# A linear-attention and mixture-of-experts kernel: reordered opening, two added products, loads spread over marks, masks earlier in the vector queue

## The chip, the cores and the metric

The kernel runs on one core of a Trainium2 chip. A core has a matrix engine (PE, with its weight loads shown as PEld), a vector engine (DVE), a scalar engine (ACT), a general engine (POOL) and a queue engine (SP) that issues most transfers. Each engine takes its instructions in the order of its own queue; semaphores order the engines among each other. The metric is device time in microseconds (us) of one execution, as a median over runs.

## The reference

Two blocks stand one after the other. The first is a delta-rule attention over 4 batches x 8 heads (32 states), 768 positions, head size 48; its output is laid out as 3072 tokens of 384 numbers. The second is a mixture of 16 experts, of which each token takes one.

```python
k_n = k / (norm(k) + 1e-06)
for t in range(768):                       # each of the 32 heads has a 48 x 48 state
    y[t]  = q[t] @ state
    v_old = state^T k_n[t]
    state = state + beta[t] * outer(k_n[t], v[t] - v_old)
x = y as (3072, 384)
g = argmax(x @ w_group); e = argmax(x @ w_expert[g])          # 4 groups of 4 experts
out[token] = softmax weight of g * softmax weight of e * (relu(x @ w1[g, e]) @ w2[g, e])
```

Everything is computed in fp32.

## The kernel before, in words

The attention goes by chunks of 32 positions: 24 chunks (`NCH`), each for all 32 heads at once (4 batches x 32 positions = 128 partitions, 8 heads along the free side). Inside a chunk the recurrence is turned into a triangular solve: the matrix of products of a chunk's keys is inverted once, and then the chunk is a few matrix products with the running state `s_bd`.

For a chunk `u` the work is:

- `gram(u)` (line 234): 32 small PE products of keys with keys and queries (line 251), copied out by ACT into `gts` (line 256, input of the inverse) and `raws` (line 262, input of the mask). In the steady loop it runs ten chunks ahead (`LEAD`).
- `inverse(g)` (line 273): one inverse for a group of four chunks (`RG`), six groups in all, almost all of it on DVE. It begins with a transpose into `m` (L279) and the start of the roots (L287, for groups after the first). The norms' roots are 14 small POOL operations (L290 to L295) for the groups 1 to 5, and DVE operations for group 0. Then come the factor (L320 to L328), a product of 1024 columns (L330), the elimination in about ninety small steps (L338 to L366), two products of 1024 columns (L369, L372), the diagonal (L374), a transpose into `mt` (L377), and eight "spreads" of `mt` into `mtb` (lines 385 to 388; all on ACT except the first one of group 0, which is DVE's, L386). `inverse` is a generator; its `yield`s say what it stands at: `ROOTS` after the POOL operations are issued, `FACTOR` after the factor, `TURN` until the group before has been transposed.
- `scale(u)` (L403, DVE): the values times the norms, into `vh` (two buffers). It needs the norms of the chunk's group and the chunk's `kv` load.
- `mask(u)` (L268, DVE): the query products times a triangle, into `gqm` (three buffers).
- `advance(u)` (line 410), four steps: `a_ps` (PE, L416 from `vh` and L422 from the state, then ACT L426 to `f`) and the first part of `o_ps` (L431); `w_ps` (L439, from `f` and `mtb`; ACT L442); the new state (`s_ps` L449, copied to `s_bd` by ACT L455); the rest of `o_ps` (L463 or L468, from `gqm`), copied to `x` by ACT L472.
- `logits(u)` and `route(r)`: the router of the chunk's 128 tokens, a sorting of tokens by expert.

The order on every engine is written out by hand: within the `manual_schedule` block the instructions stand in each engine's queue in the order in which the Python code issues them. `work(n)` (line 663) issues DVE steps of the running inverses and routes for a budget that grows with `n` and with the task's share; `allow(what)` (line 676) pushes the tasks that stand at `what`.

The opening, before the loop over the chunks (lines 689 to 723): loads of the first keys; the gram products of chunks 0 to 7; `inverse(0)` by `work` calls; `scale(0)`; three small POOL operations (`acc`, `what`, `sel`); the first step of `advance(0)` (one product, L416); the gram products of chunks 8 and 9; then `inverse(1)` is started while the end of `inverse(0)` is still being issued, and `mask(0)` and `scale(1)` are issued when `mt` of group 0 has been issued.

The loads of the opening stand in `bursts` (line 221): after the i-th gram an ACT operation writes one element of the target (a "mark", L696), and the loads issued by SP wait for the mark, since they overwrite it. The last entry, after gram 10, marks and issues the loads of keys 8 and 9, `kv` 2, the router's weights `wr`, and keys 10 and 11.

At the end of a loop period `u` (lines 829 to 836): `mask(u + 1)`, `scale(u + 2)`, the loads of keys `u + 12` and `kv` `u + 3`, then the store of `x` of chunk `u`.

After the last chunk the experts' stage goes through the 16 experts in order of their token counts (L964 first layer, L983 second layer, weights loaded ahead, tokens gathered and results scattered by POOL's indirect transfers). The change touches none of it.

## Time and profile before

| what | value |
| --- | --- |
| median of 5 runs | 518.11 us (513.5 to 520.34) |
| the profiled execution, whole | 517.32 us |
| its span, first to last instruction | 515.1 us |
| PE busy over the span | 474.1 us (92%) |
| DVE busy over the span | 250.0 us (49%) |
| first `w_ps` of chunk 0 (L439) | starts at 42.95 us |
| last `w_ps`, chunk 23 | starts at 226.54 us |
| experts' stage, first L964 in the chain | from 243.08 us |

Times inside the profile are counted from the span's start. The page cuts the span into 40 slices of 12.9 us, so that a digit string shows where an engine is busy: the opening is the first three slices and a bit, the chunks reach to about the eighteenth, and the rest is the experts' stage. A wait is given as the engine and line that waited, what it waited for, the total, how often, and the longest. "issue" stands for idle time in which the engine waited for nothing that the profile shows. Rows of the timeline give start, duration, engine, line, operation, output and inputs, and in square brackets the idle time before.

### The profile page before, as it was taken

How to read it: one execution, taken by the hardware profiler on the slowest of the kernel's cores; microseconds unless marked ns; L12 is line 12 of the kernel's file. 1: busy time of each engine (PE TensorE's matmuls, PEld its weight loads, DVE VectorE, ACT ScalarE, POOL GpSimd, SP SyncE). 2: the span in 40 equal slices, each digit the busy share in tenths (PEclk: the TensorE clock that was granted, in tenths of full speed). 3: DMA queues.
4: the chain of work that ended last, by engine and by line, in shares of the span. 5: the costliest groups of instructions: out<-in, count | busy, mean ns of one | idle time of the engine just before them, and what ended most of it. 6: DMA issues, size and time to landing. Idle time of an engine off the chain costs nothing.

```text
span 515.1 us, 18246 instructions
## 1 busy us (share of the span) xinstructions
PE 474.1 (92%) x7844; PEld 439.1 (85%) x7844; DVE 250.0 (49%) x829; ACT 188.6 (37%) x397; POOL 194.4 (38%) x288
## 2 busy tenths in 40 slices
PE   4346999999999999999999999999999999999993
PEld 3235878878888788879999999999999999999992
DVE  3999999999999994426411022012201111011110
ACT  3224767677676776742111111111111121111110
POOL 0040200623717334010345554466435644454313
PEclk9999999999999999999999999999999999999998
DMA  5781444444324545210698877779768977879641
GB/s 176 251 296 44 153 145 140 166 147 156 132 70 131 158 142 184 71 45 17 160 363 255 264 260 255 224 229 315 251 193 280 334 244 243 262 272 307 216 166 46
DMA packets 57333, 99.94 MB, mean 194 GB/s; under 512 B 18974, under 2 KB 41433, under 8 KB 57251
## 3 DMA queue, kind: packets, MB, share of 16 engines
q1 hardware_dynamic: 51331, 88.76, 52.2%
q0 software_dynamic: 5920, 10.00, 6.2%
q8 instruction: 63, 1.03, 0.8%
q14 instruction: 19, 0.16, 0.1%
HBM read 84.61 MB, written 14.27 MB: 192 GB/s over the span
## 4 chain that ended last, share of the span: by engine, by line
PE 56%; issue 12%; DMA 10%; POOL 9%; DVE 5%; ACT 5%; SPq 1%; POOLq 0%; ACTq 0%; DVEq 0%
PE y_ps L983 12%; PE h_ps L964 12%; DMA out_dram<-yo,to_i 6%; POOL xq L936 6%; PE w_ps L439 5%; PE s_ps L449 5%; ACT s_bd L455 3%; PE a_ps L422 3%; PE l_ps L500 3%; PE o_ps L431 3%; PE o_ps L463 3%; PE g_ps L251 2%; PE t_ps L490 2%; PE a_ps L416 2%; POOL out_dram L995 2%
## 5 line engine op out<-in xcount | busy, mean ns | idle before, releaser
L983 PE MATMUL y_ps<-hid,w 128*128 128x224 f32 (+15 forms) x768 | 133.3, 332 | 0.7 <-issue 0.7
L983 PEld LDWEIGHTS y_ps<-hid,w 128*128 128x128 f32 x768 | 128.9, 190 | 2.2 <-issue 1.6
L964 PE MATMUL h_ps<-xt,w 128*128 128x232 f32 (+14 forms) x720 | 122.8, 330 | 0.0
L964 PEld LDWEIGHTS h_ps<-xt,w 128*128 128x128 f32 x720 | 120.0, 190 | 0.6 <-DVE xt L930 0.4
L936 POOL DMA_INDIRECT xq<-x_dram,from_q x92 | 87.8, 955 | 34.9 <-issue 24.8
L986 DVE COPY yt<-y_ps 128x232 f32<-128x232 f32 (+13 forms) x14 | 5.1, 366 | 135.9 <-PE y_ps L983 129.5
L995 POOL DMA_INDIRECT out_dram<-yo,to_i x32 | 34.2, 1067 | 94.2 <-DVE yo L1033 85.2
L967 ACT ACTIVATE hid<-h_ps 128x448 f32<-128x448 f32 (+15 forms) x64 | 32.1, 502 | 99.9 <-PE h_ps L964 80.6
L988 ACT ACTIVATE yt<-y_ps 128x224 f32<-128x224 f32 (+15 forms) x34 | 11.5, 337 | 119.1 <-PE y_ps L983 70.5
L366 DVE TENSOR_TENSOR m<-m,t 128x81 f32<-128x81 f32 (+13 forms) x156 | 52.1, 334 | 0.0
L360 DVE TENSOR_TENSOR t<-m 128x81 f32<-128x81 f32 (+13 forms) x156 | 51.8, 332 | 0.2
L455 ACT ACTIVATE s_bd<-s_ps 48x768 f32<-48x768 f32 x46 | 37.0, 804 | 14.0 <-PE s_ps L449 13.4
L343 DVE SCALAR_TENSOR_TENSOR m<-m 128x29 f32<-128x29 f32 (+27 forms) x174 | 40.4, 235 | 0.4
L1033 DVE TENSOR_SCALAR yo<-yr,gate 128x384 f32<-128x384 f32 (+14 forms) x28 | 11.1, 417 | 52.4 <-DMA yr<-y_dram 42.7
L388 ACT ACTIVATE mtb<-mt,con 128x256 f32<-128x256 f32 x47 | 34.3, 742 | 1.4 <-DVE mt L377 1.4
L439 PE MATMUL w_ps<-f,mtb 64*64 64x48 f32 x768 | 28.4, 224 | 4.4 <-DVE mtb L386 3.7
L251 PE MATMUL g_ps<-kqt 48*32 48x64 f32 (+1 forms) x1216 | 18.6, 240 | 14.4 <-issue 9.4
L439 PEld LDWEIGHTS w_ps<-f,mtb 64*64 64x64 f32 x768 | 25.2, 138 | 6.5 <-ACT mtb L388 4.0
L251 PEld LDWEIGHTS g_ps<-kqt 48*32 48x32 f32 x1216 | 14.6, 118 | 16.5 <-issue 11.2
L422 PEld LDWEIGHTS a_ps<-s_bd,kqt 128*32 128x32 f32 x736 | 15.3, 111 | 15.5 <-ACT s_bd L455 7.3
L539 POOL TENSOR_TENSOR acc<-acc,hots 128x16 f32<-128x16 f32 x16 | 5.3, 330 | 60.1 <-DVE hots L537 59.1
L449 PE MATMUL s_ps<-w,kv 32*128 32x96 f32 x736 | 27.4, 286 | 0.2 <-issue 0.2
(159 smaller groups left out, 607.0 us busy)
## 6 DMA issues: line engine op xcount, KB each, us to landing
w<-in_w_dram SPq DMA_DIRECT2D x29, 1536.0 KB
kv<-in_kv_dram SPq DMA_DIRECT2D x24, 448.0 KB
kqt<-in_kq_dram SPq DMA_DIRECT2D x20, 512.0 KB
x_dram<-x SPq DMA_DIRECT2D x24, 192.0 KB
w<-in_w_dram SPq DMA_DIRECT2D x24, 128.0 KB
y_dram<-yq SPq DMA_DIRECT2D x36, 84.0 KB
yr<-y_dram SPq DMA_DIRECT2D x14, 192.0 KB
kqt<-in_kq_dram SPq DMA_DIRECT2D x8, 256.0 KB
```

The costliest lines, as they stand in the source:

```text
L251: nc.tensor.matmul(g_out[quads[b], hh * NP + j, of], lhsT=kqt[rows, 0, j, quads[b]], rhs=kqt[rows, of, j, quads[b]], start=True, stop=True ...
L343: nc.vector.scalar_tensor_tensor(row, in0=m[:, j, 0:j], scalar=m[:, i, j:j + 1], in1=row, op0=ALU.mult, op1=ALU.add)
L360: nc.vector.tensor_tensor(tv, m[:, j + 2:, j:j + 1].to_broadcast([128, n, j]), m[:, j:j + 1, 0:j].to_broadcast([128, n, j]), op=ALU.mult)
L366: nc.vector.tensor_tensor(below, below, tv, op=ALU.add)
L388: nc.scalar.activation(mtb[:, rows, a], from_, ACT.Copy, scale=by)
L439: nc.tensor.matmul(w_ps[b, h], lhsT=mt[b, uu * H + (h % 2) * NP + h // 2], rhs=f[b, h], start=True, stop=True, skip_group_check=True)
L449: nc.tensor.matmul(s_at[:, b, j], lhsT=k[quads[b], j], rhs=w[quads[b], 2 * j:2 * j + 2], start=(u == 0 and j == 0), stop=True, skip_group_ ...
L455: nc.scalar.activation(s_bd[rows, :, :, hh, :], s_at[rows, :, :, hh * D:(hh + 1) * D], ACT.Copy)
L936: nc.gpsimd.indirect_dma_start(out=xq[:, g, :], out_offset=None, in_=x_dram[:, :].rearrange("n (q c) -> (n q) c", q=4), in_offset=bass.Ind ...
L964: nc.tensor.matmul(h_ps[:, k], lhsT=w1[:, j, (f + k) * 128:(f + k + 1) * 128], rhs=xt[:, j, 0:R], start=(j == 0), stop=(j == DC - 1), skip ...
L983: nc.tensor.matmul(y_ps, lhsT=w2[:, f, j * 128:(j + 1) * 128], rhs=hid[:, f], start=(f == 0), stop=(f == FC - 1))
L995: put = nc.gpsimd.indirect_dma_start(out=out[:, :], out_offset=bass.IndirectOffsetOnAxis(ap=to[0:P, i:i + 1], axis=0), in_=yo[0:P, :], in_ ...
```

## The change

Six edits, all in the opening and in the order of a few DVE and SP instructions of the loop.

- In the opening the first two spreads of group 0 (one on DVE, one on ACT) are issued before anything of `inverse(1)`. Only then come, on DVE: the transpose and the start of the roots of group 1, `mask(0)`, `scale(1)`, `mask(1)`, `scale(2)`, `mask(2)`, and then the factor of group 1, which needs POOL's roots.
- POOL's three small operations (`acc`, `what`, `sel`) stand behind the roots of group 1, and no longer ahead of them.
- After the gram of chunk 9, PE does two products of the identity with a constant (128x128 by 384 columns, fp32, the shape of L416) into `s_ps`. Nobody reads them.
- The last burst of loads is cut up: keys 8 and 9 as before; keys 10 and `kv` 2 behind marks after the gram of chunk 8; keys 11 and `wr` behind marks after `w_ps` of chunk 0.
- In the loop `mask(u + 1)` is issued at the beginning of period `u` (from `u` = 2), and no longer at its end; on DVE's queue it thereby moves from just ahead of `scale(u + 2)` to just behind `scale(u + 1)`.
- In period 0 the loads of keys 12 and `kv` 3 are issued behind the store of `x` of chunk 0.

On the queues, this is all that moves: PE has four more matmul instructions of L416's kind, ACT the moved marks and one mark more, DVE and POOL the same instructions in another order, SP the same transfers in another order.

```diff
-                         (kv_[2], [lambda: load_kv(2),
-                                   lambda: nc.sync.dma_start(out=wr, in_=wr_d)])]
-            + [of_kq(u) for u in range(2 * RG + 2, NB)],
         }
+        after_gram = [of_kq(2 * RG + 2), (kv_[2], [lambda: load_kv(2)])]
+        after_w = [of_kq(2 * RG + 3), (wr[:, 0], [lambda: nc.sync.dma_start(out=wr, in_=wr_d)])]
...
             scale(0)
+            ahead = advance(0)
+            next(ahead)
+            for u in range(2 * RG, LEAD):
+                gram(u, homes[u % len(homes)])
+                if u == 2 * RG:
+                    begin(after_gram)
+            for _ in range(2):
+                nc.tensor.matmul(s_ps[:, 0, 0:H * D], lhsT=ident, rhs=cut["below"][:, 0:H * D],
+                                 start=True, stop=True, skip_group_check=True)
+            while 0 not in mts:
+                work(4)
+                allow(ACT_STEP)
+            second = inverse(1)
+            start(second, 0.95)
+            while held.get(second) is not ROOTS:
+                work(2)
+            mask(0)
+            scale(1)
+            mask(1)
+            scale(2)
+            mask(2)
+            allow(ROOTS)
+            while held.get(second) is not FACTOR:
+                work(2)
+            allow(FACTOR)
             nc.gpsimd.memset(acc[:, 0], 0.0)
...
-            ahead = advance(0)
-            next(ahead)
-            for u in range(2 * RG, LEAD):
-                gram(u, homes[u % len(homes)])
-            start(inverse(1), 0.95)
-            made = 0
-            while 0 not in mts:
-                work(4)
-                if 1 not in vhs and 0 in turned_over:
-                    mask(0)
-                    scale(1)
-                allow(ACT_STEP)
-                made += 1
-                if made == LAST:
-                    allow(ROOTS)
-            allow(FACTOR)
...
+                if 1 < u < NCH - 1:
+                    mask(u + 1)
                 if u:
                     next(step)
...
                 next(step)
+                if u == 0:
+                    begin(after_w)
                 for v in ahead_of[u]:
                     gram(v)
...
-                if u + 1 < NCH:
-                    mask(u + 1)
-                if u + 2 < NCH:
+                if 0 < u < NCH - 2:
                     scale(u + 2)
-                if u + NB < NCH:
+                if 0 < u < NCH - NB:
                     load_kq(u + NB)
-                if u + NV < NCH:
+                if 0 < u < NCH - NV:
                     load_kv(u + NV)
...
                     nc.sync.dma_start(out=x_dram[1 + u * 128:1 + (u + 1) * 128], in_=xs[u])
+                if u == 0:
+                    load_kq(NB)
+                    load_kv(NV)
```

`begin(burst)` is the former loop body as a function: for each pair, the mark on ACT and then its loads.

More of the change, by code (lines that the diff above doesn't have):

```diff
@@ L20 @@
 FIXED, TILE = 1, 128
-LAST = 8
 SLOTS = [224] * FIXED + [232, 220, 214, 208, 204, 202, 200, 198, 194, 190, 186, 184, 180, 174, 168]
@@ L225, in deltanet_then_moe @@
             2 * RG: [(kv_[0], [lambda: load_kv(0), lambda: load_con(2), lambda: load_kv(1)])],
-            2 * RG + 2: [of_kq(2 * RG), of_kq(2 * RG + 1),
-                         (kv_[2], [lambda: load_kv(2),
-                                   lambda: nc.sync.dma_start(out=wr, in_=wr_d)])]
-            + [of_kq(u) for u in range(2 * RG + 2, NB)],
-        }
+            2 * RG + 2: [of_kq(2 * RG), of_kq(2 * RG + 1)],
+        }
+        after_gram = [of_kq(2 * RG + 2), (kv_[2], [lambda: load_kv(2)])]
+        after_w = [of_kq(2 * RG + 3), (wr[:, 0], [lambda: nc.sync.dma_start(out=wr, in_=wr_d)])]
         rooted = sm.tile([128, 1], F32, tag="rooted", name="rooted", bufs=1)
@@ L689, in deltanet_then_moe, with begin @@
             nc.scalar.activation(rooted, cut["tiny"], ACT.Exp)
+            def begin(burst):
+                for late, loads in burst:
+                    nc.scalar.activation(late[:, 0:1], cut["tiny"], ACT.Copy)
+                    for load in loads:
+                        load()
             homes = [None, s_ps[:, 0:2], s_ps[:, 2:4]]
@@ L694, in deltanet_then_moe @@
                 gram(u, homes[i % len(homes)], parts)
-                for late, loads in bursts.get(i, ()):
-                    nc.scalar.activation(late[:, 0:1], cut["tiny"], ACT.Copy)
-                    for load in loads:
-                        load()
+                begin(bursts.get(i, ()))
             start(inverse(0), 1)
```

## The prediction

> **What bounds the kernel now.** First the page: the span, and the digit strings of the 40 slices.

> ```profile
> span 515.1 us, 18246 instructions
> ...
> PE   4346999999999999999999999999999999999993
> ...
> DVE  3999999999999994426411022012201111011110
> ```

> PE is full from the fourth slice to the end, so PE's start and stalls seem to set the time. But DVE is full too, from 10 to 198 us. For whether one waits for the other I read the waits: PE's in the opening (0 to 43 us), PE's from 43 to 245 us, then DVE's from 10 to 198 us (columns: who, for whom, total us, times, longest).

> ```profile
> PE g_ps L251 <- issue: 8.6, 3, 4.9
> ```
> ```profile
> PE w_ps L439 <- DVE mtb L386: 3.7, 1, 3.7
> PE a_ps L422 <- ACT s_bd L455: 1.8, 9, 0.4
> PE g_ps L251 <- issue: 0.8, 2, 0.5
> ```
> ```profile
> DVE m L279 <- ACT gt L256: 7.5, 1, 7.5
> DVE what L601 <- POOL cw L575: 0.5, 2, 0.2
> DVE r L320 <- POOL nrm L295: 0.5, 1, 0.5
> ```

> PE's idle time before 43 us shows under "issue" and for the first spread. From 43 us on PE almost never waits, and from 10.04 us on DVE doesn't either: some 1.0 us of waits in 188 us. Both are saturated, and PE runs a little behind DVE. How little, two pairs of timeline rows show: `vh` of chunks 5 and 17 (DVE, L403), and the product that reads it (PE, L416).

> ```profile
> 79.38 0.55 DVE L403 TENSOR_TENSOR vh<-kv,normt 128x384 f32<-128x384 f32 x1
> ...
> 82.49 0.91 PE L416 MATMUL a_ps<-vh,con 128*128 128x384 f32 x2
> ...
> 175.02 0.55 DVE L403 TENSOR_TENSOR vh<-kv,normt 128x384 f32<-128x384 f32 x1
> ...
> 177.46 0.91 PE L416 MATMUL a_ps<-vh,con 128*128 128x384 f32 x2
> ```

> Chunk 5's is done 2.56 us ahead of its reader (82.49 less 79.93), chunk 17's 1.89 us (177.46 less 175.57). The same subtraction gives 7.9, 6.5, 4.1, 3.1 us for chunks 1 to 4 and 2.9 us or more for the others; group 5's transpose ends at 195.38 and ACT's first spread of it starts at 197.59 us, 2.2 us. **So PE can't gain more than 1.89 us by chunk 17 unless DVE gains too.** That decides the case.

> **Part by part.** *First spread ahead of the second inverse.* These rows of the timeline are the end of the opening:

> ```profile
> 36.17 1.34 POOL L293 TENSOR_TENSOR r<-r,r 128x32 f32<-128x32 f32 x1
> 36.19 1.22 DVE L369 TENSOR_TENSOR cs<-con,r 128x1024 f32<-128x1024 f32 x1
> ...
> 39.13 0.35 DVE L320 RECIPROCAL r<-nrm 128x32 f32<-128x32 f32 x1 [0.46 <-POOL nrm L295]
> ...
> 42.95 1.95 PE L439 MATMUL w_ps<-f,mtb 64*64 64x48 f32 x32 [3.74 <-DVE mtb L386]
> ```

> Ahead of the transpose `mt` DVE loses L279 and L287 of group 1 (1.15 + 0.11), the wait for POOL (0.46) and the factor (L320 to L328, 0.92): 2.64 us. Ahead of DVE's own spread `mask(0)` and `scale(1)` go too (0.57 + 0.47): 3.68 us. ACT's half (L388, 41.45 to 42.19 us) follows the transpose and ends 2.64 us sooner, at 39.55, DVE's at 39.12. The first `w_ps` could start at 39.6 instead of 42.95 us.

> *The two products* stand ahead of it on PE. L416's pair at 31.30 us took 1.65 us, the same pair at 82.49 us 0.91: PE ran at half pace until 52 us (the granted clock reads 1.00 there too, so only the durations tell). Two cold products are 3.3 us. Chunk 9's gram, ahead of them, lost 2.88 us to "issue" and ended at 39.21. With that stall unchanged `w_ps` starts at 42.5 us; with none the products end at 39.6. I take the 1.60 us of the like stall at 30.70 us (fewer loads were then in flight, as now): about 41.2 us, a gain of 1.7. Warm, chunk 0's rows would fall from 1.95, 1.5, 2.04, 1.94 and 1.65 (L439, L251, L449, L463, L416) to chunk 1's 1.14, 0.86, 1.15, 1.14 and 0.91, some 3.9 us, and chunk 1's L422 from 1.19 to 0.87, 4.2 in all. PE's early gain is so 0.5 to 7.5 us (3.3 + 4.2), by these values 5.9.

> *What DVE pays.* The roots of group 1 (14 POOL operations) ran from 32.40 to 39.09 us beside `inverse(0)`, and DVE lost 0.46 us. Now they start only after L279 and L287 of group 1 (39.12 + 1.26 = 40.4 us), and DVE has but `mask(0)`, `scale(1)`, `mask(1)`, `scale(2)`, `mask(2)` beside them, 2.7 us, until 43.1. POOL's cadence while DVE does small operations is 0.335 us, so 14 take at least 4.7 us: 45.1. The slowest of the five recorded chains took 7.13 us: 47.5. I take 5.6 us (46.0), near the 5.31 us of group 2's chain, which met one mask and one scale; L293 above shows a POOL operation held to the end of a long DVE one. DVE so waits 2.9 us (2.0 to 4.4) where it waited 0.46. The three operations moved ahead (1.65 us) are saved later and cost nothing net. POOL's copies (L705, L706) stretched an L366 at 28.80 us to 0.78 us, 0.4 us over its like; they now meet L330. I take half of that as gained. **DVE is later by 2.9 - 0.46 - 0.2 = 2.2 us** (2.0 - 0.46 - 0.4 = 1.1, to 4.4 - 0.46 = 3.9) from `inverse(1)` on, with nothing after it to make that up: its queue holds the same instructions and no idle time.

> *Masks.* `mask(3)` was ready 1.6 us and `mask(4)` 2.0 us ahead of L463, the others 3 us and more. They come a period earlier in the queue, so this limit goes, but `vh` has the same instructions ahead of it as before and is not moved. The buffers it needs are free when the `vh` ahead of it can be written. Gain: nothing; without it chunk 3 would wait for its mask.

> *Loads.* Keys 8 and 9 are alone in flight, and so the gram's wait may shrink (counted above). `kv` 2, read by `scale(2)` at about 42 us, is issued behind gram 8's ACT copies (ended 34.92 us) and is there by 39: in the trace the seven transfers of this burst took until 39 us in all. Keys 11 and 12 and `kv` 3 are issued between 42 and 47 us; the first reader is chunk 1's gram, 55 us before. SP's queue behind the store of `x` holds only these. Nothing, and 0.4 us of marks on ACT in chunk 0, hidden under PE.

> [...]

> [...]

> **The sum.** PE would reach chunk 3's L416 5.9 us sooner (66.51 - 5.9 = 60.6 us), but its `vh` comes at 62.44 + 2.2 = 64.7 us: PE waits 4 us. At chunk 4 it waits again (`vh` at 71.86 + 2.2 = 74.1), at chunk 5 it stands at 82.2 against 82.49, and at chunk 17 `vh` ends at 177.8 against a start of 177.46. What is left is 2.2 - 1.89 = **0.3 us later**, with DVE's bounds 0.8 us sooner to 2.0 us later. The experts' stage follows one to one. Against the profiled execution that is 517.32 + 0.3 = 517.6 us; the median shown is 0.8 us above that execution, which gives 518.4. I say 518.1, between the two.

> **Rivals.** *Slower, the clock closes at chunk 3.* PE, early and warm, idles 4 us there for `vh`. At 226.8 to 230.1 us it was busy 2.35 of 3.3 us, and the granted clock from 230.2 to 233.5 us was 0.50: such a stretch costs 1.7 us, and the opening stayed cold for 10 us of work (42.95 to 52.6), which cost 4.2. Chunk 4's wait hides 1.9 us, the distance at chunk 5 some 0.3; from there it counts. One long closing is 2.0 us late on top of 518.4, a second one at chunk 5 makes 6.2: 520.4 to 524.6 us. Against: once PE is behind DVE again it has no gaps, so it ends by itself. 0.22.

> *Faster, the early gain arrives.* Then DVE's wait must be hidden or its work shorter, and PE keeps 0.8 to 5.9 us: 512.2 to 517.3 us. Against: no idle DVE time is on record to absorb it. For: executions from 513.5 to 520.34 us show that some luck exists. 0.15.

> *It does not do what it says:* the stall of chunk 9's gram stays and the products don't warm PE. `w_ps` starts at 42.5 us; DVE still decides, 518.4 us. 0.05.

> The forecast itself (517.3 to 520.1 us) gets 0.58. About 1% (5.2 us) is what a measurement of this kernel can tell from no change. Faster by more needs the last fifth of the second rival and of the spread of medians: 0.05. Slower by more than that (over 523.3 us) is the dearest third of the first rival: 0.08. Within: 0.87. The range, 513.5 to 522.5 us, leaves out the ends of both rivals.

> **What would show it.** Right: `w_ps` starts between 39.6 and 42.5 us; DVE's wait of L320 for L295 rises from 0.46 to 2 us or more; new waits of PE's L416 for `vh` at chunks 3 and 4, summing to several us; chunk 17's L416 within 1 us of 177.5. Wrong: no such waits, or `vh` of chunk 5 ending before 80 us; then DVE was not late. A granted clock of 0.50 between 60 and 80 us would be the first rival.

## The result, and the profile after

The changed kernel takes 521.21 us (median of 27 runs, 515.64 to 526.31), the kernel before 516.87 us in the same session (53 runs, 512.87 to 522.34). The ratio is 1.0064, with a 95% interval of 1.0042 to 1.0086: **slower by 0.64%, some 3.3 us.** That is inside the 1% that the prediction called no change, and inside its range (513.5 to 522.5), but it is not the forecast, which was 0.06%. (The ratios leave out each kernel's slowest, disturbed runs; the medians keep them, so that a ratio of medians comes out a little larger.)

The loss is not in every execution. Of the changed kernel's 29 executions whose granted PE clock is on record, the six with a mean clock of 0.986 or more took 516.3 to 517.6 us, like the kernel before; the other 23 have a median of 522.2 us.

The page of the changed kernel, whose profiled execution took 524.2 us, one of its longer ones:

```profile
span 521.9 us, 18259 instructions
...
PE   4378899999899999999999999999999999999993
...
DVE  2997999999999995514611122012201111011110
...
PEclk9997989999789999997999999999999999999998
```

DVE has a dent in the fourth slice (7 where it had 9). PE fills the third slice and the fourth more than before, but has dents in the fifth and the eleventh. The last string is new: the granted clock falls below full speed in the fourth, sixth, eleventh, twelfth and nineteenth slice. The kernel before has 9 in all but the last. I call a stretch at half clock (0.50) a closing. The closings of this execution before the kernel's end last 6.83, 3.41, 10.24 and 6.83 us, the one of the kernel before 3.41: all are 3.41 us or a multiple of it, and I call 3.41 us a window.

DVE's waits from 10 to 205 us, and PE's from 40 to 260 us (who, for whom, total us, times, longest):

```profile
DVE r L318 <- POOL nrm L293: 3.1, 1, 3.1
```
```profile
PE a_ps L414 <- DVE vh L401: 2.0, 2, 1.8
PE a_ps L420 <- ACT s_bd L453: 1.8, 9, 0.3
PE s_ps L619 <- POOL at L559: 1.7, 1, 1.7
```

(Line numbers of the attention are two lower than before: L318 is the former L320, L414 the former L416, L619 the former L621.) The first row is the wait for the roots that the prediction put at 2.9 us; before it was 0.5. The second is PE's new wait for `vh`. The last row was not in the prediction: PE's sorting product (L619, it brings a chunk's tokens into the order of the experts) waits for `at`, a table that POOL makes (L559).

Since that execution is a long one, I read the steps in another one too: `e17`, the same changed kernel run again (517.56 us). Its DVE wait is the same 3.1 us. What the two share is what the text relies on.

Up to chunk 11 DVE goes as forecast, and PE's early gain comes in part only. In the execution of 524.2 us the first `w_ps` starts at 39.2 us (42.95 before), and PE is ready for chunk 3 at 63.42 us, 3.1 us sooner than before. `vh` of chunk 5 ends at 82.60 us (79.93), so DVE is 2.7 us late, and PE waits at chunk 3:

```profile
62.29 1.13 PE L461 MATMUL o_ps<-w,gqm 64*64 64x48 f32 x32
65.22 0.91 PE L414 MATMUL a_ps<-vh,con 128*128 128x384 f32 x2 [1.80 <-DVE vh L401]
```
```profile
82.05 0.55 DVE L401 TENSOR_TENSOR vh<-kv,normt 128x384 f32<-128x384 f32 x1
```

In `e17` the first `w_ps` starts at 39.4 us, but then the clock is closed from 54.09 to 60.91 us. PE comes to chunk 3 at 66.28 us, only 0.2 us sooner than before (66.51), and waits for `vh` 0.3 us at chunk 4 and 0.4 us at chunk 5.

PE's L414 of chunk 11 starts at 130.92 us (130.85 in `e17`) against 131.42 before: the early gain and the late DVE have cancelled, with half a microsecond left over. Then the two part. These are PE's rows at that place, first of the kernel before, then of the changed one (`e17`; rows left out at the dots):

```profile
133.72 0.55 PE L490 MATMUL t_ps<-con,x 128*128 128x128 f32 x3
134.10 0.54 PE L621 MATMUL s_ps<-mine,at 128*128 128x48 f32 x4
...
136.43 1.15 PE L449 MATMUL s_ps<-w,kv 32*128 32x96 f32 x32
```
```profile
133.15 0.55 PE L488 MATMUL t_ps<-con,x 128*128 128x128 f32 x3
135.12 0.65 PE L619 MATMUL s_ps<-mine,at 128*128 128x48 f32 x4 [1.42 <-POOL at L559]
...
138.46 2.04 PE L447 MATMUL s_ps<-w,kv 32*128 32x96 f32 x32
```

Why `at` is late, the same two kernels' POOL rows tell:

```profile
130.08 1.12 POOL L295 TENSOR_SCALAR nrm<-r 128x32 f32<-128x32 f32 x1
131.30 0.92 POOL L561 TENSOR_SCALAR at<-con,place 128x256 f32<-128x256 f32 x1
```
```profile
132.93 1.12 POOL L293 TENSOR_SCALAR nrm<-r 128x32 f32<-128x32 f32 x1
134.15 0.92 POOL L559 TENSOR_SCALAR at<-con,place 128x256 f32<-128x256 f32 x1
```

On POOL's queue this `at` stands behind the roots of the next group (`nrm` is their last operation). The roots start when DVE has reached that group, and DVE is late, so `at` ends at 135.07 us and not at 132.22. Before, it was there 1.88 us ahead of its reader (134.10 less 132.22). An `at` 2.85 us later and a PE 0.57 us earlier use that up and leave some 1.5 us, of which the row shows 1.42 as waiting.

The wait is the smaller part of the price. `e17` in windows (columns: window, its length, busy us and instructions of PE, PEld, DVE, ACT, POOL, granted clock, DMA share, GB/s):

```profile
132.59:136.00 3.41, 1.99 (x49) 1.56 (x40) 3.24 (x7) 0.98 (x2) 3.06 (x7) 1.00 0.57 181
136.00:139.42 3.42, 3.42 (x111) 3.16 (x109) 3.15 (x10) 1.30 (x3) 2.81 (x6) 0.50 0.03 8
139.42:142.83 3.41, 3.41 (x48) 3.19 (x42) 3.38 (x17) 2.16 (x4) 3.18 (x4) 0.50 0.36 108
142.83:146.24 3.41, 3.41 (x45) 2.24 (x46) 3.41 (x13) 1.41 (x3) 0.00 (x0) 0.50 0.24 91
```

After a window in which PE was busy for 1.99 of 3.41 us the granted clock reads 0.50 for three windows. L447 takes 2.04 us in them instead of 1.15. Chunk 12's `w_ps` starts at 148.0 us (143.0 before): with the 0.57 us that PE was ahead and 1.42 of waiting, the closing cost 5.0 + 0.57 - 1.42 = 4.2 us. Nothing gives it back: chunk 23's `w_ps` starts at 231.6 us (226.5). In the execution of 524.2 us the same closing lasts from 137.85 to 148.09 us, and a further one, at the end of the chunks, from 236.84 to 243.67. The kernel before has a closing at the end of the chunks too, of one window (230.14 to 233.55), and `e17` has none there. For the most part that is why its experts' stage begins 2.35 us late (L964 before at 242.91, L980 after at 245.26) and not 5.1. The experts' stage itself, which no edit here touches, took 270.1 to 275.7 us in the profiles (e9 and e10 aside), so that profiles are best compared by the start of chunk 23's `w_ps`, ahead of it.

### The profile page after: what moved, and what is told of

It is laid out like the page before. It is cut to its first block, busy times and chain, and to the rows that moved or that the text cites. A ratio compares the mean times of both kernels' runs of the same rounds, so it can differ in the third digit from the quotient of the medians.

```text
span 521.9 us, 18259 instructions
## 1 busy us (share of the span) xinstructions
PE 483.3 (93%) x7848; PEld 446.6 (86%) x7848; DVE 250.0 (48%) x829; ACT 189.0 (36%) x398; POOL 193.1 (37%) x288
## 4 chain that ended last, share of the span: by engine, by line
PE 41%; DVE 21%; DMA 17%; issue 7%; POOL 5%; SPq 4%; ACT 4%; DVEq 0%; POOLq 0%; ACTq 0%
PE y_ps L999 12%; PE h_ps L980 12%; DMA y_dram<-yq 6%; DMA out_dram<-yo,to_i 5%; DVE t L358 5%; DVE m L364 5%; DMA yr<-y_dram 5%; SPq L1039 4%; DVE m L341 3%; ACT s_bd L453 3%; PE s_ps L447 2%; PE w_ps L437 2%; PE l_ps L498 2%; PE a_ps L420 2%; PE x_ps L740 2%
## 5 line engine op out<-in xcount | busy, mean ns | idle before, releaser
L980 PE MATMUL h_ps<-xt,w 128*128 128x232 f32 (+14 forms) x720 | 122.8, 330 | 0.8 <-DMA w<-in_w_dram 0.8
L980 PEld LDWEIGHTS h_ps<-xt,w 128*128 128x128 f32 x720 | 120.1, 190 | 1.3 <-PE y_ps L999 1.1
L386 ACT ACTIVATE mtb<-mt,con 128x256 f32<-128x256 f32 x47 | 34.1, 739 | 1.1 <-DVE mt L375 1.1
L288 POOL TENSOR_TENSOR r<-r 128x32 f32<-128x32 f32 x15 | 5.9, 393 | 65.7 <-DVE r L285 64.9
L447 PE MATMUL s_ps<-w,kv 32*128 32x96 f32 x736 | 28.7, 293 | 0.0
```

The costliest lines, as they stand in the source:

```text
L386: nc.scalar.activation(mtb[:, rows, a], from_, ACT.Copy, scale=by)
L447: nc.tensor.matmul(s_at[:, b, j], lhsT=k[quads[b], j], rhs=w[quads[b], 2 * j:2 * j + 2], start=(u == 0 and j == 0), stop=True, skip_group_ ...
L980: nc.tensor.matmul(h_ps[:, k], lhsT=w1[:, j, (f + k) * 128:(f + k + 1) * 128], rhs=xt[:, j, 0:R], start=(j == 0), stop=(j == DC - 1), skip ...
```

## The experiments

Ratios are to the kernel before in the same session; its median was 517.5 to 518.5 us in three sessions, and 512.8 to 513.3 us in three others.

### Which part of the change costs

**e1: the roots of group 1 started before the first spread, all else as changed.** DVE does the transpose and the start of the roots of group 1 ahead of the first spread again, and POOL's chain has the rest of `inverse(0)` beside it.

```diff
+            second = inverse(1)
+            start(second, 0.95)
             while 0 not in mts:
                 work(4)
                 allow(ACT_STEP)
-            second = inverse(1)
-            start(second, 0.95)
```

> The changed kernel, but the transpose and the start of the roots of group 1 (L277, L285) are issued during the end of the first inverse, as in the kernel before; the factor, the masks and the scales stay behind the first spread. Theory A (the exposed wait of the vector engine for POOL's roots makes it 2.7 us late, PE then meets POOL's late `at` and the clock closes): the wait of the reciprocal for the roots falls from 3.1 us to under 0.5 us, the first spread comes 1.3 us later than in the changed kernel (about 40.5 us), `vh` of chunk 5 ends at 80 us or sooner and no longer at 82.6, and the time is 0.994 to 1.001 of the kernel before. Theory B (the opening on PE is at fault: products, loads, the clock opening early and closing again): nothing of that is undone here, the time stays at 1.004 to 1.009.

Measured: ratio 0.9983 (0.9948 to 1.0019), and DVE's wait is not there; its waits, from 10 to 205 us, are

```profile
DVE m L277 <- ACT gt L254: 7.9, 1, 7.9
...
DVE what L599 <- POOL cw L573: 0.5, 2, 0.2
```

`vh` of chunk 5 ends at 79.2 us, sooner than in either kernel, and the first `w_ps` still starts at 41.0 us. The loss is gone with DVE's wait. PE, now 3.2 us ahead of the kernel before at chunk 11, does wait for `at` in this profile, but the clock stays open behind that wait (L447 takes its 1.15 us):

```profile
132.17 0.65 PE L619 MATMUL s_ps<-mine,at 128*128 128x48 f32 x4 [1.14 <-POOL at L559]
...
134.60 1.15 PE L447 MATMUL s_ps<-w,kv 32*128 32x96 f32 x32
```

So a wait for `at` of 1.1 us does not close the clock every time.

**e2: the changed kernel without the two idle products.**

```diff
-            for _ in range(2):
-                nc.tensor.matmul(s_ps[:, 0, 0:H * D], lhsT=ident, rhs=cut["below"][:, 0:H * D],
-                                 start=True, stop=True, skip_group_check=True)
```

> The changed kernel without the two idle products. Theory A: the vector engine is as late as with them, `vh` of chunk 3 ends at 65 us and PE waits less for it since it stays cold longer; the time is 1.003 to 1.009 of the kernel before. Theory B (the products open the clock early, PE then starves and it closes): 0.998 to 1.002, and a first opening near 50 us as in the kernel before.

Measured: 1.0059 (1.0022 to 1.0096), DVE's wait 3.1 us, `vh` of chunk 5 at 82.4. The products are not the cause: without them the loss is as large. Its profile, an execution of 517.65 us, shows another way to pay: no wait for `at` at chunk 11, but, besides the closing behind chunk 3's wait, another one (75.25 to 78.66 us) behind 0.9 us of "issue" in chunk 3's last product, after which chunk 5's L414 starts at 84.41 us, 1.9 us later than before.

**e3: the kernel before, with nothing of the change, but DVE kept busy by eight products at the end of the opening.**

```diff
+            idle = wk.tile([128, C * C // 4], F32, tag="t", name="idle")
+            for _ in range(8):
+                nc.vector.tensor_tensor(idle, cut["places"], cut["places"], op=ALU.mult)
```

> The kernel before, with eight vector products of 256 columns (about 2.6 us) into a scratch tile ahead of the body of the second inverse, and nothing else of the change. Theory A: the vector engine is late by 2.6 us with no part of the change in it, the sort matmul of chunk 11 (1.9 us of slack before) and the product of chunk 17 (1.9 us) wait for some 0.7 us each, the clock closes in some executions, and the time is 1.002 to 1.008 of the kernel before. Theory B: the vector engine has room, 0.999 to 1.001.

Measured: 1.0056 (1.0021 to 1.0091), `vh` of chunk 5 at 82.6 us. A late DVE is enough; no other part of the change is needed for a loss of this size. Among PE's waits from 40 to 225 us is one that the changed kernel doesn't have:

```profile
PE o_ps L463 <- DVE gqm L268: 2.1, 2, 1.6
```

With DVE late and the masks at their old place PE waits for a mask, and that is what the masks' earlier place takes away. So e3 does not pay in the changed kernel's way: in this execution the sorting product waited 0.5 us only, and the clock closed twice, both times at the end of the chunks (223.1 to 226.5 and 233.3 to 236.7 us).

**e8: e1 with the loads in one burst, as before.**

```diff
-            2 * RG + 2: [of_kq(2 * RG), of_kq(2 * RG + 1)],
+            2 * RG + 2: [of_kq(2 * RG), of_kq(2 * RG + 1),
+                          (kv_[2], [lambda: load_kv(2),
+                                    lambda: nc.sync.dma_start(out=wr, in_=wr_d)])]
+            + [of_kq(u) for u in range(2 * RG + 2, NB)],
...
-                if u == 2 * RG:
-                    begin(after_gram)
...
-                if u == 0:
-                    begin(after_w)
```

> The kernel with the early roots, with the bulk loads of the opening in one burst as in the kernel before. If the spreading of the loads matters only for PE's waits in the opening, these waits rise (the one in chunk 9's gram back to near 2.9 us), the first `w_ps` comes about 1 us later, and the time stays that of the early roots, 0.995 to 1.002 of the kernel before, since the vector engine decides. If the loads matter for more, over 1.003.

Measured: 1.0026 (0.9993 to 1.0059), beside 0.9985 (0.9946 to 1.0024) of e5 in the same session. The first `w_ps` starts at 42.5 us, against 41.0 in e1, and in the opening the gram products' waits for "issue" come to 9.7 us here and 6.2 and 6.7 us in e5 and e1. In the profiles the spread loads are worth some 1.5 us of PE's start. Nothing of it is left at chunk 23, whose `w_ps` starts at 224.4 us here and at 224.9 in both e1 and e5, and the intervals of the times overlap: a gain in time from the loads is not shown.

### Where the lateness is paid

**e4: the changed kernel with the sorting products moved behind the new state (L447), where `at` has more time.**

```diff
-                if u < NCH:
+                if NCH - 4 <= u < NCH:
...
+                if u < NCH - 4:
+                    allow(SORT)
```

> The changed kernel with the sort matmuls of chunks up to 19 issued behind the router's product in the period, some 4 us later on PE, and no longer ahead of `w_ps`. Theory A, with the wait for POOL's `at` as what closes the clock in mid-run: no wait of the sort matmul for `at` any more (1.7 us and 0.2 us before), no closing near chunk 11, and the time 0.998 to 1.003 of the kernel before, what is left being the waits for `vh` at chunks 3 to 5 and 17. If the closings come from the waits for `vh` alone, 1.004 to 1.009 as the changed kernel.

Measured: 1.0385 (1.0335 to 1.0435), a miss. The sorting product writes the tile of the running state, `s_ps`, and so it had to wait for ACT's copy of the state:

```profile
PE s_ps L619 <- ACT s_bd L453: 5.6, 5, 1.1
```

Five waits of 1.1 us are 5.6 us, but the kernel lost 20. The clock closed seven times between 64 and 178 us. The move was a bad one, and it shows stalls of 1 us that keep coming back, with a clock that keeps closing.

**e5 and e6: POOL's four `at` of a route issued together, ahead of the next group's roots; e5 in e1, e6 in the changed kernel.**

```diff
-            elif not final:
+            if early or not final:
                 for u in us:
                     turn_to(u)
             for g, u in enumerate(us):
-                if early:
-                    turn_to(u)
```

> The kernel with the early roots of the first experiment, and the four `at` tiles of a group issued on POOL together, ahead of the next group's roots, and no longer one by one. Theory A: the wait of the sort matmul for `at` (1.1 us with the early roots) goes, no clock window closes near 130 us, and the time is 0.993 to 0.998 of the kernel before. If this wait is not what closes the clock: as with the early roots alone, 0.996 to 1.001.

> The changed kernel (late roots) with the four `at` tiles of a group issued together. Theory A1 (most of the loss comes through POOL's late `at`): no wait of the sort matmul, chunk 12 starts 0.5 us ahead of the kernel before or level with it, 0.999 to 1.003 of the kernel before. Theory A2 (the waits of PE for `vh` at chunks 3 to 5 close the clock, and that is most of the loss): closings at 60 to 85 us stay, 1.003 to 1.007.

Measured: e5 0.9985 (0.9946 to 1.0024), no gain over e1's 0.9983; e6 1.0050 (1.0014 to 1.0087). In both profiles the sorting product waits no longer and the clock stays open from 71 to 229 us. In e6 PE then is where it was before the change: chunk 16's `w_ps` starts at 173.7 us in both. Yet e6 stayed slower. Its profile lost the time at the end of the chunks, where the clock was closed from 230.63 to 240.87 us, three windows instead of one, and the experts' stage began at 247.03 us. So the wait for `at` is not all of it. Nor is that closing shown to come from the late DVE: e5, whose DVE is not late, was closed there for three windows too (229.03 to 239.27 us).

**e7, e11 and e14: one idle product (224 columns) ahead of the last chunk's `r_ps`, where PE waits for small steps of the router.** e7 is e5 with it, e14 is e7 again, e11 is the kernel before with it.

```diff
+                if u == NCH - 1:
+                    nc.tensor.matmul(x_in[0][:, B - 1, 0:224], lhsT=ident, rhs=cut["below"][:, 0:224],
+                                     start=True, stop=True, skip_group_check=True)
```

> The previous-but-one kernel (early roots, `at` together) with one more idle product, identity by 224 columns, on PE ahead of the router's product of the last chunk, where PE waits about 1 us around 229 us. If the closing of the clock at the end of the attention (one window in the profiles of the kernel before, of the changed kernel and of the one without products) comes from that idle time, the mean clock rises by 0.002 to 0.003 and the time falls by 1 to 1.7 us against that kernel, to 0.990 to 0.996 of the kernel before; if not, no difference.

> The kernel before with this one idle product at the end of the attention and nothing else. If the gain of the earlier kernel with the filled tail was the tail's alone, 0.996 to 0.999 of the kernel before, with the mean clock up from 0.989 by 0.001 to 0.003; if it came from the early opening too, 0.999 to 1.001.

> e7_tail_filled word for word, beside other runs of the kernel before. If it does beat the kernel before: ratio 0.994 to 0.999, as then (0.9966). If that was chance: 0.999 to 1.003.

Measured: e7 0.9966 (0.9938 to 0.9995), e14 0.9940 (0.9912 to 0.9968), e11 1.0006 (0.9984 to 1.0029). **The version of e7 and e14 is faster than the kernel before, in two sessions.** Its gain is not shown to come from the idle product: e5, without it, lies inside e7's interval, e11 gained nothing, and in the profiles of e7 and e14 the clock still closed for one window at that place. e11's profile also shows that closings are not the changed kernel's alone: up to that product it is the kernel before, and its clock was closed from 75.40 to 78.81 us, behind 0.7 us of "issue" that the kernel before has at the same place without a closing.

### The clock, or the lateness itself

**e9 and e10: the changed kernel with idle products where PE waits for `vh` (six at chunk 3, three at chunk 4); e10 with e7's product too.**

```diff
+                for _ in range({3: 2, 4: 1}.get(u, 0)):
+                    nc.tensor.matmul(s_ps[:, 1, H * D:512], lhsT=ident, rhs=cut["below"][:, 0:128],
+                                     start=True, stop=True, skip_group_check=True)
...
```

(and the same for `s_ps[:, 2]` and `s_ps[:, 3]`.)

> The changed kernel with idle products on PE where it waits for the late `vh`: six of identity by 128 columns (1.7 us) ahead of chunk 3's first product, three (0.85 us) ahead of chunk 4's, into unused columns of `s_ps`. The vector engine stays late by 2.7 us. Theory C (what costs is the clock that closes while PE waits; the lateness itself is worth only 2.7 less 1.9 us of slack, 0.8 us or 0.16%): no closing between 60 and 90 us, the mean clock over the executions rises from 0.978 to 0.983 or more, and the time is 1.001 to 1.004 of the kernel before. Theory D (the lateness itself costs the 3.3 us): 1.004 to 1.009 as the changed kernel, whatever the clock.

> The kernel just described with one more idle product of 224 columns ahead of the router's product of the last chunk, where PE waits at the end of the attention. Theory C: the mean clock rises further, to 0.985 to 0.990, and the time is 0.998 to 1.002 of the kernel before. Theory D: 1.004 to 1.009.

Measured: 1.0745 and 1.0768. These times say nothing on the question: in the two profiles the experts' stage took 308 us where it takes 272 in the changed kernel's, so it had other work. The router works from the output of the running state. That the idle products, with the start flag and in columns of `s_ps` beside the state's, upset the state is the author's reading; no trace shows the state itself.

**e12 and e13: the same with `start=False`.**

> The changed kernel with idle products of PE behind chunk 3's (six) and chunk 4's (three) last part of o_ps, where PE waits for vh, now without the start flag, so that the state is untouched. 0.23 us each warm: 1.4 and 0.7 us of work. Both theories: no wait of L414 over 1 us at chunks 3 and 4, and no closed clock there in most executions; vh of chunk 5 still ends at 82 to 83 us. Closed clocks cost the changed kernel most of its loss (C): ratio 1.001 to 1.004, median clock 0.983 to 0.988 (changed kernel: 0.978, before: 0.989). Lateness of DVE costs it, whatever the clock does (D): ratio 1.004 to 1.009.

> As the run before, and one idle product of 224 columns ahead of the last chunk's r_ps, where the clock closed in several profiles near 230 us. C: ratio 0.998 to 1.002, median clock 0.985 to 0.990. D: 1.003 to 1.009, and within 0.002 of the run before.

Measured: 1.0030 (0.9990 to 1.0070) and 1.0082 (1.0050 to 1.0115); e12's executions spread from 515.30 to 525.54 us; the experts' stage takes 272 and 273 us in the two profiles. The question stayed open, since the fill was too small: at chunk 3 six products took 1.6 us, and PE still waited 1.9 us. In both profiles the clock closed behind that wait, and again behind a wait of 2.0 us for `at`, and at the end of the chunks.

**e15 and e16: the changed kernel with the `at` together and the product at the end (e6 and e7's edits); e15 with twelve idle products at chunk 3 and three at chunk 4, e16 with none of these.** Their difference, on e12's lines:

```diff
-                for _ in range({}.get(u, 0)):
+                for _ in range({3: 4, 4: 1}.get(u, 0)):
```

> The changed kernel with twelve idle products where PE waits for vh of chunk 3 (in e12 six of them took 1.6 us and a wait of 1.9 us was left, so twelve leave 0.3 to 0.6) and three at chunk 4, POOL's four `at` of a route issued together (which takes the wait of the sorting product at 134 us away, as in e6), and one idle product of 224 columns ahead of the last chunk's r_ps. DVE stays late: vh of chunk 5 at 82 to 83 us. Closed clocks cost the changed kernel its loss (C): no window at half rate between 60 and 150 us in the profile, median clock 0.984 or more, ratio 0.996 to 1.002. Lateness costs it whatever the clock does (D): 1.003 to 1.009.

> The same kernel without the idle products at chunks 3 and 4, the rest as in the run before it. C: ratio 1.004 to 1.008, a closed window behind chunk 3's wait, median clock 0.976 to 0.980. D: the same as the run before it within 0.002.

Measured: 1.0016 (0.9988 to 1.0044) and 1.0012 (0.9985 to 1.0039). Chunk 3's wait in windows of e15, and then of e16:

```profile
62.13:65.55 3.42, 3.07 (x25) 2.88 (x26) 3.38 (x12) 0.48 (x2) 2.00 (x6) 1.00 0.34 131
65.55:68.96 3.41, 3.41 (x99) 2.55 (x99) 3.41 (x17) 0.98 (x2) 2.75 (x9) 1.00 0.10 17
```
```profile
62.01:65.43 3.42, 0.44 (x2) 0.30 (x2) 3.38 (x12) 0.28 (x1) 2.19 (x6) 1.00 0.32 123
65.43:68.84 3.41, 3.41 (x66) 2.44 (x64) 3.38 (x17) 0.49 (x1) 2.37 (x9) 0.50 0.00 0
```

The idle products keep the clock open (PE busy 3.07 us, then 1.00), without them PE is busy 0.44 us and the next window runs at 0.50. **And it makes no difference:** chunk 5's L414 starts at 82.8 us in e15 and at 82.5 in e16. Chunk 4's wait for `vh` hides the whole closing. DVE is late by 2.8 us in e15 and by 2.5 in e16, and both ratios are within 0.2% of the kernel before (their intervals end at 1.0044 and 1.0039). So neither the lateness by itself nor the closed clock at chunk 3 costs what the changed kernel loses: each theory's ratio for one of the two runs failed. Chunk 17 in e16, DVE's `vh` and PE's product from it:

```profile
177.10 0.54 DVE L401 TENSOR_TENSOR vh<-kv,normt 128x384 f32<-128x384 f32 x1
...
177.79 0.88 PE L414 MATMUL a_ps<-vh,con 128*128 128x384 f32 x2 [0.23 <-DVE vh L401]
```

**e17 and e18: the changed kernel itself, and e16 again, side by side.**

> The changed kernel as it is, beside e18 on one chip. Theory C2: lateness alone costs at most 0.3 us once PE is behind DVE again (e16 showed chunk 17 within 0.15 us), and one closed window behind chunk 3's wait is hidden by chunk 4's; what costs is every later closing (behind the sorting product's wait at 134 us and at the end of the chunks), 1.7 us for each window of 3.41 us. Then this kernel is 1.004 to 1.009 and its median clock 0.004 or more below that of the kernel before, and it is 0.003 or more above e18. If the difference between the sessions is the chip's (D2), both come out alike, within 0.002 of each other.

> e16_no_fill word for word: the changed kernel with POOL's four `at` issued together and one idle product at the tail. C2: 0.998 to 1.003 wherever the clock then stays open, a clock within 0.003 of that of the kernel before. D2: like e17, within 0.002.

Measured: e17 1.0046 (1.0012 to 1.0080), e18 1.0013 (0.9986 to 1.0041); medians 515.62 and 513.76 us, 1.9 us apart; e17's fastest execution (513.99) is slower than eight of e18's twelve. Seven executions of e17, with a clock of 0.986 or more, took 514.0 to 516.3 us, the other five 517.6 to 520.4; the profile is of one of the five. At the place where e17 waits for `at`, e18 has

```profile
134.64 0.55 PE L488 MATMUL t_ps<-con,x 128*128 128x128 f32 x3
135.03 0.54 PE L617 MATMUL s_ps<-mine,at 128*128 128x48 f32 x4
...
137.35 1.15 PE L447 MATMUL s_ps<-w,kv 32*128 32x96 f32 x32
```

no wait, and L447 at its warm 1.15 us. That is the edit's doing, for POOL's roots end no sooner than in e17 (134.05 us):

```profile
133.68 1.11 POOL L293 TENSOR_SCALAR nrm<-r 128x32 f32<-128x32 f32 x1
```

An `at` of 0.92 us behind them would have ended at 135.7 us or later, and its reader starts at 135.03. Its experts' stage begins at 241.41 us, e17's at 245.26. The expected distance of 0.003 came (0.0033, though the two intervals against the kernel before overlap). Of the expected clocks e17's came, 0.987 against 0.994 in the kernel before; e18's did not, since it is 0.987 too. e18 has closings as well, from 37.88 to 48.12 us and behind chunk 3's wait, but these are followed by a wait for DVE, which hides them. In these two profiles it is the place of a closing that counts, not the number of closings. The two kernels differ by two edits, the `at` together and the product at the end; the times do not separate them, the profiles put the difference at `at`.

The start of chunk 23's `w_ps` sums up the profiles. It is 226.5 us in the kernel before. With a late DVE, a wait of 1.4 to 2.0 us for `at` and a closing behind it (the changed kernel, e12, e13, e17) it is 230.3 to 232.1; with a late DVE and the `at` together (e6, e15, e16, e18) 227.0 to 227.7; with the roots early (e1, e5, e7, e8, e14) 223.8 to 225.6.

## Why the prediction was wrong, and where it was right

1. **First spread and early gain.** The start was right: the first `w_ps` came at 39.2 and 39.4 us, just below the interval of 39.6 to 42.5. The gain was smaller than the 5.9 us forecast: PE was ready for chunk 3's L414 4.8 us sooner in e16 (61.75 against 66.51 us), 3.1 us in the execution of 524.2 us, and 0.2 us in e17, whose clock had closed on the way. Since PE waits for DVE behind it, that changed nothing in the sum.
2. **DVE's wait for the roots.** Right: 3.1 us for 2.9. DVE's lateness was 2.7 us at chunk 5 for 2.2: the wait was 0.2 longer, and the 0.2 credited for POOL's copies did not show.
3. **Masks: nothing, without the move chunk 3 would wait for its mask.** Right by e3, whose wait for `gqm` is 1.6 us.
4. **Loads: nothing but the start.** In line with e8, not shown by it.
5. **PE waits at chunks 3 and 4, and chunk 17's slack decides.** Forecast were a wait of 4 us at chunk 3 and a further one at chunk 4; the changed kernel's profiles have 2.0 and 0.7 us in all, by the smaller gain. The rest is right where the clock stays open from chunk 5 on and `at` is early: in e16 chunk 17's `vh` ends at 177.64 us (177.8 forecast) and PE waits 0.23 us for it, and the last `w_ps` starts 0.5 us later than before (227.0 against 226.5; 0.3 forecast).
6. **"DVE still decides", the sum of 0.3 us. This is the step that failed**, because of a path that it left out. The slack was taken for one reader of DVE alone, PE's product from `vh`. A second path goes from DVE over POOL's roots to POOL's `at` and to PE's sorting product, and its slack at chunk 11, 1.88 us, is as small as chunk 17's 1.89, which was called the smallest. It is used up first: with DVE late by the forecast's own 2.2 us the sorting product would already wait 0.3 us, and with `at` 2.85 us later and PE half a microsecond early it waited 1.4 us. What follows is dearer than the wait: in e17 4.2 us by three windows at half clock, for which the sum had no term. It does not follow each time (e1's wait of 1.1 us, the executions with a clock of 0.986 or more).
7. **The rival "the clock closes at chunk 3"**, at 0.22, had the mechanism right and place and price wrong. The clock did close behind chunk 3's wait, in nine of the twelve profiles that have the changed opening with its late DVE. But there it costs nothing (e15 against e16), since chunk 4's wait absorbs it (chunk 5's L414 starts at 82.8 us with the clock open, at 82.5 with it closed); e2's second closing, 10 us later, left PE 1.9 us late at chunk 5. The price of 2.0 us and more that this rival named is paid in the changed kernel at 136 us, where no wait for DVE follows. That 521.2 us lies in this rival's range (520.4 to 524.6) is so in part luck. The argument against it, "once PE is behind DVE again it has no gaps", is what failed.

What stays open is how the 3.3 us divide. That a late DVE is their cause is shown by e1, e2 and e3 in one session; by which way it is paid is read from profiles of single executions. Behind the wait for `at` some 5.6 us go (1.4 of waiting, 4.2 of closed clock), less the half microsecond that PE was ahead, in an execution in which the clock closes there. But e6 has no wait for `at` and is still at 1.0050, while e16 and e18, at 1.0012 and 1.0013, differ from it by the product at the end and by the session; no run separates these two. e6's profile puts the time at the end of the chunks, and e5's closing there, as long, goes with a ratio of 0.9985. Why the clock stays closed there for one window in some executions, for two or three in others, and not at all in the profiles of e1, e11 and e15 to e18, no run here tells; the product put there did not settle it (e13 has it, and three windows).

## What to carry to other kernels

When an engine is made late on purpose, list the slack of everybody who follows it, also of those who follow it over the queue of a third engine, and take the smallest of all; here the smallest was behind two hand-overs. The price of a stall of PE lay in what came after it: where PE had to wait again soon, a closed clock was free (e16, chunk 5's L414 at 82.5 us, against 82.8 in e15 with the clock open), and where PE was the limit from there on, a stall of 1.4 us cost 5.6 (e17). And issue a chain's first link before the work that shares its engine: started before the first spread, POOL's roots cost DVE no wait that the profile lists (e1; 3.1 us in the changed kernel), and the change without that wait, with the `at` issued together and the idle product at the end, is 0.3 to 0.6% faster than the kernel before.

## What the runs showed of the hardware

```profile
42.28:45.69 3.41, 3.21 (x63) 2.87 (x64) 0.83 (x2) 1.54 (x3) 2.68 (x10) 0.50 0.41 146
45.69:49.11 3.42, 3.42 (x47) 2.25 (x47) 2.80 (x8) 2.75 (x5) 1.18 (x5) 0.50 0.00 0
```

- **Idle products into unused columns of `s_ps`, with the start flag, went with a longer experts' stage:** 308 us in e9 and e10, against 272 and 273 in e12 and e13, which differ from them in that flag alone.
- **The kernel before ran at 518 us in some sessions and at 513 in others**, with a median granted clock of 0.989 to 0.990 and of 0.994. Only ratios inside a session can be compared.
